# Attention and expert layer on one core: the second pair's x operands are issued eight slots later, behind six project blocks

## The chip, the cores and the metric

The kernel runs on one core of a Trainium2 chip. A core has TensorE (PE, the matmuls; PEld is its weight load), VectorE (DVE), ScalarE (ACT), GpSimd (POOL) and SyncE (SP, which here only issues DMAs). Each of them works through its own instructions in the order in which they were written; semaphores tie them together. The metric is the device time of one execution, in microseconds (us). One execution was also profiled, and the rows below are from it.

## The reference

Two layers follow each other. The first is attention with a learned bias (4 batches, 8 heads, 576 positions, 64 wide), the second a feed-forward layer on its 2304 tokens:

```
attn = softmax(scale * q @ k.T + bias(|i - j|)) @ v        # x: 2304 tokens x 512
h = x @ w_in                                               # 512 -> 2048
g = s * max(h, 0)**2 + b
out = g @ w_out                                            # 2048 -> 512
```

All is float32. The kernel multiplies in a reduced format (fp32r) and keeps the precision by splitting each operand into a high part and a low part, so that each product is three matmuls: high x high, high x low, low x high.

## The kernel before

The attention part fills the first 261 us; it is left as it is, but for two sums at its very end. The feed-forward part follows and is laid out in **slots**. An **item** is a pair of a weight group g (4 of them, 512 of the 2048 hidden columns each) and a token pair p (3 of them, 768 tokens each, which are two blocks of 384 columns). `items` (L465) is their order: (0, 0), (0, 1), (0, 2), (1, 2) and so on, twelve in all. The text calls p = 0, 1, 2 the first, second and third pair, and the items with them the first, second and third item.

The product with w_in is done by a Strassen scheme: 7 products in place of 8, on sums of blocks of x (T1 to T4, `X_SUMS`) and of w (S1 to S4). Each of the 7 needs an **x operand**, numbered 1 to 7: a block of x or one of the sums T1 to T4, split by `x_hi` (L593, on ACT, two instructions) and `x_lo` (L596, on DVE, two instructions). `x_sum` (L582) makes a sum, two instructions on DVE. `store_x` writes an operand to DRAM for later items, `load_x` reads a pair's x.

An item is two halves of seven slots, 14 slots in all. In slot T the loop at L1104 issues, in this order: one `product` (L625, six matmuls of 384 columns), in the order 1, 6, 5, 7, 2, 3, 4; then, by `SHARE`, some **project blocks** of the half before (`project`, L732: three matmuls of 512 columns each, twelve blocks a half); then `fire(T)`, which issues all that was put down for that slot with `at(slot, fn, prio)`, by priority (0 first, x work has 2). The four banks of PSUM hold a: products 1 and 2, b: 5 and 3, c: 6, d: 7 and 4. The work behind a half is `quad_posts` (L640), slots 1 to 9 after the half's start: ACT copies bank a (L657, slot 1), DVE adds c (L661, slot 2), adds b (L666, slot 3, the text calls it **v**), adds d (L669, slot 4); then relu (L680, L687), square, scale (L699), a high part (L707) and a low part (L716) for each of four blocks, which `project` reads. Product 3 adds into bank b in slot 5 of a half and so has to wait until v has read it. `evict` takes a finished output block from PSUM, on ACT for the first weight group.

The first item has no project blocks of a half before it, so its 14 slots are 84 matmuls of 384 columns and nothing else. The x operands of the first pair are made ahead of it (`prep`). Those of the second pair were made by `fresh_x(0, 1, ...)` in slots 6 to 14, that is while the first item runs, and those of the third pair by `fresh_x(1, 2, ...)` in slots 20 to 28, while the second item runs. Decoding of the next weight group (`fresh_w`, L491 to L501) lies beside it, on ACT, POOL and DVE.

```
        for o, name in ((6, "T1"), (7, "T2"), (9, "T3"), (12, "T4")):
        for i, m in enumerate(ORDER):
            o = base + (7 + i if i > 0 else 6)      # x_hi at o, x_lo at o + 1
    SHARE = (0, 4, 0, 0, 4, 0, 4)
```

## Time and profile before

| what | value |
|---|---|
| median of 3 runs | 648.07 us (647.71 to 653.99) |
| the profiled execution | 650.64 us |
| its span, first to last instruction | 648.9 us |
| PE busy | 631.1 us, 97% |
| DVE busy | 511.4 us, 79% |
| ACT busy | 450.9 us, 69% |
| mean granted clock of PE | 0.994 |

The profile names an instruction by its line, its engine and its tiles (out<-in); a start is counted from the first instruction of the span, "idle before" is how long the engine stood still ahead of it, and the arrow behind it names what it waited for. Matmuls are pipelined: they start closer together than one lasts, so a rate is read from the starts. In a group of equal instructions the time runs from the first start to the last end. The granted clock is given as a share of full speed: 1.00 is 2.4 GHz, 0.50 is 1.2 GHz.

### The profile page before, as it was taken

Reading aid. Unit: us, or ns where it says so; the run is one execution under the profiler, and the core shown is the slowest. Engines: PE = TensorE matmul, PEld = TensorE weight load, DVE = VectorE, ACT = ScalarE, POOL = GpSimd, SP = SyncE. Lnnn points to the kernel's source line nnn. Section 1 sums busy time; section 2 is a strip of 40 time slices with the busy share of each in tenths; the row PEclk is TensorE's granted clock in tenths of the full one; section 3 lists DMA queues with packets and bytes.
Section 4 is the critical chain, followed back from the end, with each engine's and each line's share of the span. In section 5 each row is a group of like instructions: output and inputs, shape, how many; then the busy total and the mean of one; then the engine's idle time right before and its main releaser. Section 6 shows DMA issues by size and latency. Waiting matters only on the chain.

```text
span 648.9 us, 14523 instructions
## 1 busy us (share of the span) xinstructions
PE 631.1 (97%) x5418; PEld 511.6 (79%) x5418; DVE 511.4 (79%) x1093; ACT 450.9 (69%) x945; POOL 165.6 (26%) x196
## 2 busy tenths in 40 slices
PE   8999999999999999979999999999999999999997
PEld 5667666666666666879898899999888999998886
DVE  7988889999999988897887566698686698575542
ACT  7988787888888788687676685576574665655540
POOL 7991423345697524010010100010100100000000
PEclk9999999999999999979999999999999999999999
DMA  6988777775776565693522445421627210718112
GB/s 187 327 249 248 260 245 236 246 235 183 255 245 220 170 205 159 219 368 110 223 92 89 168 164 177 164 88 34 239 95 251 90 58 1 268 48 280 62 48 98
DMA packets 51058, 115.27 MB, mean 178 GB/s; under 512 B 10156, under 2 KB 18860, under 8 KB 50988
## 3 DMA queue, kind: packets, MB, share of 16 engines
q1 hardware_dynamic: 50652, 114.08, 52.6%
q8 instruction: 43, 0.70, 0.4%
q10 hardware_dynamic: 208, 0.26, 0.1%
q14 instruction: 27, 0.22, 0.1%
q0 software_dynamic: 128, 0.00, 0.0%
HBM read 83.59 MB, written 30.14 MB: 175 GB/s over the span
## 4 chain that ended last, share of the span: by engine, by line
PE 75%; DMA 7%; POOL 5%; ACT 5%; DVE 4%; issue 3%; SPq 1%; DVEq 0%; ACTq 0%; POOLq 0%
PE o L741 31%; PE hps L635 27%; PE bps L168 5%; PE xps L437 5%; PE sps L275 4%; PE tps L348 3%; ACT pr L308 3%; DMA qt<-in_q_dram 2%; DMA kt<-in_k_dram 2%; DVE tt L297 1%; DMA rs<-rt 1%; POOL kr L248 1%; DMA big<-in_moe_w_in_dram 1%; DVE pt L378 1%; ACT pt L376 1%
## 5 line engine op out<-in xcount | busy, mean ns | idle before, releaser
L741 PE MATMUL o<-wo,gt 128*128 128x512 f32 x864 | 209.2, 392 | 0.0
L635 PE MATMUL hps<-x,wi 128*128 128x384 f32 x1008 | 190.7, 340 | 3.3 <-DVE h L666 3.3
L635 PEld LDWEIGHTS hps<-x,wi 128*128 128x128 f32 x1008 | 180.8, 190 | 10.0 <-DVE h L666 3.6
L741 PEld LDWEIGHTS o<-wo,gt 128*128 128x128 f32 x864 | 161.2, 188 | 31.3
L308 ACT ACTIVATE pr<-tt,mn 128x576 f32<-128x576 f32 x144 | 110.7, 770 | 35.4 <-DVE mn L297 35.2
L297 DVE CUSTOM_DVE_ANT_0 tt<-sps,bt 128x576 f32<-128x576 f32 x128 | 91.4, 751 | 8.4 <-PE sps L275 6.7
L348 PEld LDWEIGHTS tps<-ident,pr 64*128 64x128 f32 x1216 | 44.8, 137 | 44.2 <-issue 18.7
L437 PE MATMUL xps<-pt,vt 128*64 128x256 f32 (+1 forms) x512 | 76.0, 418 | 1.0 <-PE xps L437 1.0
L275 PE MATMUL sps<-kr,qr 64*128 64x288 f32 x768 | 73.2, 307 | 1.0 <-POOL kr L248 0.8
L348 PE MATMUL tps<-ident,pr 64*128 64x64 f32 x1216 | 56.7, 229 | 5.2 <-ACT pt L376 2.8
L275 PEld LDWEIGHTS sps<-kr,qr 64*128 64x128 f32 x768 | 58.8, 186 | 2.4 <-POOL kr L248 1.0
L699 ACT ACTIVATE h<-h,sb 128x384 f32<-128x384 f32 x72 | 50.8, 706 | 12.0 <-DVE h L695 10.8
L493 POOL TENSOR_SCALAR wf<-wf 128x512 f32<-128x512 f32 x16 | 13.0, 813 | 160.8 <-ACT wf L491 160.6
L378 DVE COPY pt<-tps 128x512 f32<-128x512 f32 x64 | 43.9, 685 | 9.1 <-PE tps L348 8.8
L680 ACT ACTIVATE h<-hps 128x384 f32<-128x384 f32 x24 | 11.7, 487 | 54.5 <-PE hps L635 54.5
L437 PEld LDWEIGHTS xps<-pt,vt 128*64 128x64 f32 x512 | 31.3, 136 | 21.3 <-issue 9.4
L716 DVE TENSOR_TENSOR gt<-h,gt 128x384 fp32r<-128x384 f32 x72 | 40.0, 557 | 6.1 <-ACT gt L707 6.0
L168 PE MATMUL bps<-f,pt__125 128*32 128x79 f32 (+44 forms) x640 | 39.7, 390 | 2.0 <-POOL f L137 1.2
L707 ACT ACTIVATE gt<-h 128x384 fp32r<-128x384 f32 x72 | 37.9, 526 | 2.3
L135 DVE TENSOR_SCALAR f<-lg,thr 128x432 f32<-128x432 f32 (+9 forms) x68 | 39.3, 659 | 0.0
L168 PEld LDWEIGHTS bps<-f,pt__125 128*32 128x32 f32 x640 | 24.1, 109 | 17.7 <-issue 6.4
L376 ACT ACTIVATE pt<-tps 128x512 f32<-128x512 f32 x64 | 36.8, 575 | 0.0
(145 smaller groups left out, 823.6 us busy)
## 6 DMA issues: line engine op xcount, KB each, us to landing
x<-xs SPq DMA_DIRECT2D x24, 768.0 KB
bias<-stg SPq DMA_DIRECT2D x36, 295.5 KB
xs<-x SPq DMA_DIRECT2D x12, 768.0 KB
bt<-bias SPq DMA_DIRECT2D x7, 1152.0 KB
kt<-in_k_dram SPq DMA_DIRECT2D x16, 464.0 KB
wd<-in_moe_w_out_dram SPq DMA_DIRECT2D x12, 512.0 KB
x<-xt SPq DMA_DIRECT2D x28, 192.0 KB
qt<-in_q_dram SPq DMA_DIRECT2D x16, 320.0 KB
```

Of the source, the lines that this page charges most:

```text
L168: nc.tensor.matmul(pb[32 * c:32 * c + 32, base + a:base + b], w2bd, mov, start=True, stop=True)
L275: nc.tensor.matmul(o, a, b, start=(i == 0), stop=(i == 2))
L297: nc.vector.tensor_tensor_reduce(tt.rearrange("p (a b) -> p a b", a=2), ps[x][:, :, 0:HALF], bias.rearrange("p (a b) -> p a b", a=2), -1.0 ...
L308: nc.scalar.activation(pr[:, x], tts.pop((n, x)), AF.Exp, bias=mn[:, x:x + 1], scale=-1.0, accum_out=sums[p][:, col // 3, col % 3:col % 3 ...
L348: nc.tensor.matmul(outs[r], src[d], ident[d, d], is_transpose=True, start=start, stop=True, skip_group_check=not start)
L376: nc.scalar.activation(o, i, AF.Copy)
L378: nc.vector.tensor_copy(o, i)
L437: nc.tensor.matmul(o, vt[:, 4 * x + kb, :], pt[:, kb, x, c], start=(i == 0), stop=(i == 4))
L635: nc.tensor.matmul(ps, w_ops[m][:, w, k, s], xo[p, m][:, x, k], start=(first and i == 0), stop=(i == 5), skip_group_check=not first)
L699: return lambda: nc.scalar.activation(tmp[fo, j], tmp[fo, j], AF.Identity, bias=b_, scale=s_)
L716: nc.vector.tensor_tensor(lo, tmp[fo, j], hi, op=ALU.subtract)
L741: nc.tensor.matmul(os_t[t], gt[:, a, tok], w[:, b], start=(fo == 0 and i == 0), stop=(fo == 3 and i == 2))
```

## The change

The second pair's operands are now issued in slots 12 to 19 by a new list of (slot, sum or operand), the third pair's in slots 23 to 30. T1 of the second pair is issued ahead of the last step of the attention part. A new helper `x_make` issues the two high parts and the two low parts of an operand in one slot. At slot 14, where the second item starts, six project blocks of the first item's first half are issued ahead of its product 1, those of fo = 1 first; the other six follow three at a time in slots 16 and 18. `project` therefore starts an output block with whichever of its blocks comes first. The loads of the third pair's x go from slot 16 to slot 19, and the first six decode steps of the second weight group from slots 15 to 20 to slots 19 to 22. What is computed stays the same.

```diff
@@ -729,17 +729,21 @@
 
     BLOCKS = [(t, fo) for fo in (0, 1) for t in range(3)] + [(t, fo) for t in range(3) for fo in (2, 3)]
 
+    begun = set()
+
     def project(n, j, k):
         g, p = items[n]
         t, fo = BLOCKS[k]
-        if fo == 0:
+        begin = (n, j, t) not in begun
+        if begin:
+            begun.add((n, j, t))
             os_t[t] = ps_o.tile([128, DM], F32, tag="o", name="o")
         gt = gts[n, fo, j]
         tok = slice(128 * t, 128 * t + 128)
         w = w_outs[fo]
         for i, (a, b) in enumerate(((0, 0), (0, 1), (1, 0))):
             nc.tensor.matmul(os_t[t], gt[:, a, tok], w[:, b],
-                             start=(fo == 0 and i == 0), stop=(fo == 3 and i == 2))
+                             start=(begin and i == 0), stop=(fo == 3 and i == 2))
         if (t, fo) in ((2, 0), (2, 1), (2, 2), (2, 3)):
             free_g.append(gts.pop((n, fo, j)))
 
@@ -971,6 +975,13 @@
         for e in range(2):
             x_lo(0, m, e, x_free[e])
 
+    def x_make(q, m, free):
+        x_new(q, m)
+        for e in range(2):
+            x_hi(q, m, e)
+        for e in range(2):
+            x_lo(q, m, e, free)
+
     next(att)
     for a in range(KB):
         load_x(1, a, 0, 2 * CH if a < KB - 1 else CH)
@@ -989,6 +1000,11 @@
         prep(m)
     product(0, 0, 1, False)
     product(0, 0, 6, False)
+    mix["acc"] = [tp.tile([128, 640 if i < 3 else 576], F32, tag="vn" if i < 3 else "tt", name=f"acc{i}")
+                  for i in (0, 1, 3, 4, 5)]
+    sums1 = [t[:, 0:CH] for t in mix["acc"]]
+    x_sum(1, "T1", 0, nc.vector, sums1)
+    x_sum(1, "T1", 1, nc.vector, sums1)
     next(att)
     store_xt(NP - 1)
     copy_x()
@@ -1006,8 +1022,8 @@
     free_g.extend(op.tile([128, 2, CH], F32R, name=f"gt{i}") for i in range(9))
     free_x.append(op.tile([128, 2, 2, CH], F32R, name="x7"))
     s2 = op.tile([128, 2, 2, 128], F32, name="s2")
-    mix["acc"] = [tp.tile([128, 640 if i < 3 else 576], F32, tag="vn" if i < 3 else "tt", name=f"acc{i}")
-                  for i in range(6)]
+    mix["acc"].insert(2, tp.tile([128, 640], F32, tag="vn", name="acc2"))
+    sums1.append(mix["acc"][2][:, 0:CH])
     ps_o = ctx.enter_context(tc.tile_pool(name="ps_o", bufs=4, space=PSUM, reuse_waits="tile"))
     fulls = [tp.tile([128, 576], F32, tag="rb", name=f"f{i}", bufs=2)[:, 0:512] for i in range(2)]
     free_f[:] = fulls + new_f
@@ -1015,35 +1031,27 @@
                         for i in range(2)]
     raws = [big[:, i] for i in range(4)]
     free_raw[:] = raws
-    x_free[:] = [[t[:, 0:CH] for t in mix[e]] for e in ("acc", "acc2")]
 
     for n in range(1, NI + 1):
         for j in range(2):
             for t, o in enumerate((5, 7, 7)):
                 at(14 * n + 7 * j + o, lambda n=n, j=j, t=t: evict(n - 1, 1 - j, t), 0)
 
-    def fresh_x(n, q, free):
-        base = 14 * n
-        for a in range(KB) if q > 1 else ():
-            at(base + 2, lambda a=a: load_x(q, a))
-        for o, name in ((6, "T1"), (7, "T2"), (9, "T3"), (12, "T4")):
-            for e in range(2):
-                at(base + o, lambda name=name, e=e: x_sum(q, name, e, nc.vector, free))
-        for i, m in enumerate(ORDER):
-            o = base + (7 + i if i > 0 else 6)
-            at(o, lambda m=m: x_new(q, m))
-            for e in range(2):
-                at(o, lambda m=m, e=e: x_hi(q, m, e))
-            for e in range(2):
-                at(o + 1, lambda m=m, e=e: x_lo(q, m, e, free))
-            if isinstance(X_OPS[m], str):
-                at(o + 2, lambda m=m: store_x(q, m))
+    def fresh_x(q, free, slots):
+        for o, e in slots:
+            for x in range(2):
+                if isinstance(e, str):
+                    at(o, lambda e=e, x=x: x_sum(q, e, x, nc.vector, free))
+            if not isinstance(e, str):
+                at(o, lambda e=e: x_make(q, e, free))
+                if isinstance(X_OPS[e], str):
+                    at(o + 2, lambda e=e: store_x(q, e))
 
     def fresh_w(g):
         base = 42 * (g - 1)
         first = g == 1
         if first:
-            passes = [15 + k for k in range(6)] + [28 + k // 2 for k in range(6)]
+            passes = [19 + (2 * k) // 3 for k in range(6)] + [28 + k // 2 for k in range(6)]
         else:
             passes = [base + 8 + (22 * k) // 12 for k in range(12)]
         passes += [base + 33 + k for k in range(12)]
@@ -1085,8 +1093,11 @@
     for i, m in enumerate(ORDER):
         if isinstance(X_OPS[m], str):
             at(4 + i // 2, lambda m=m: store_x(0, m), 1)
-    fresh_x(0, 1, x_free[0])
-    fresh_x(1, 2, x_free[1])
+    fresh_x(1, sums1, ((12, 1), (13, "T2"), (14, 6), (15, 5), (15, "T3"), (16, 7), (17, 2), (18, "T4"), (18, 3), (19, 4)))
+    for a in range(KB):
+        at(19, lambda a=a: load_x(2, a))
+    fresh_x(2, [t[:, 0:CH] for t in mix["acc2"]],
+            ((23, "T1"), (23, 1), (25, "T2"), (25, 6), (26, 5), (26, "T3"), (27, 7), (28, 2), (28, "T4"), (29, 3), (30, 4)))
     for g in range(1, NG):
         fresh_w(g)
     for n in range(2, NI - 1):
@@ -1101,14 +1112,19 @@
                     at(o + 4, lambda p1=p1, m=m: split_lo(p1, m))
 
     SHARE = (0, 4, 0, 0, 4, 0, 4)
+    AHEAD = 6
     for T in range(14 * NI + 15):
         n, r = divmod(T, 14)
         s, i = divmod(r, 7)
+        if T == 14:
+            for k in (3, 4, 5, 0, 1, 2):
+                project(0, 1, k)
         if n < NI and T >= 4:
             p = items[n][1]
             product(n, s, ORDER[i], s == 1 and n + 1 < NI and items[n + 1][1] != p)
         if 0 < n <= NI:
-            for k in range(sum(SHARE[:i]), sum(SHARE[:i + 1])):
+            share, k0 = ((0, 0, 3, 0, 3, 0, 0), AHEAD) if T < 21 else (SHARE, 0)
+            for k in range(k0 + sum(share[:i]), k0 + sum(share[:i + 1])):
                 project(n - 1, 1 - s, k)
         fire(T)
     sched.__exit__(None, None, None)
```

Three places in the new order carry the prediction. The first is DVE in the first item, up to v of its second half (L666). Before, sums into acc tiles and the low parts of x7 and x0 (operands 1 and 6 of the second pair) stand ahead of it:

```order
L585 TENSOR_TENSOR acc2_5389<-wd_5187,acc0_5387 128x384
L585 TENSOR_TENSOR acc3_5390<-wd_5187,acc1_5388 128x384
L598 TENSOR_TENSOR x7_5385<-wd_5187,x7_5385 128x384 x2
L716 TENSOR_TENSOR gt2_5378<-h2_5263,gt2_5378 128x384
L661 TENSOR_TENSOR h0_5261<-hps_5455,h0_5261 128x384
L716 TENSOR_TENSOR gt3_5379<-h1_5262,gt3_5379 128x384
L585 TENSOR_TENSOR acc4_5391<-wd_5187 128x384
L585 TENSOR_TENSOR acc5_5392<-wd_5187 128x384
L598 TENSOR_TENSOR x0_5180<-acc2_5389,x0_5180 128x384
L598 TENSOR_TENSOR x0_5180<-acc3_5390,x0_5180 128x384
L666 TENSOR_TENSOR h0_5261<-hps_5469,h0_5261 128x384
```

Now, at the same place:

```order
L716 TENSOR_TENSOR gt0_5383<-h2_5263,gt0_5383 128x384
L714 SCALAR_TENSOR_TENSOR gt1_5384<-h2_5263,sb_122,gt1_5384 128x384
L716 TENSOR_TENSOR gt2_5385<-h2_5263,gt2_5385 128x384
L661 TENSOR_TENSOR h0_5261<-hps_5449,h0_5261 128x384
L716 TENSOR_TENSOR gt3_5386<-h1_5262,gt3_5386 128x384
L666 TENSOR_TENSOR h0_5261<-hps_5461,h0_5261 128x384
```

Eight instructions of x work have left the piece, and v follows the low part of gt3 at once.

The second is ACT around slots 13 to 16 of the changed kernel; x0 is operand 6 and x1 operand 5 of the second pair, and hps_5533 is bank a of the second item, which its product 1 in slot 14 fills:

```order
L699 ACTIVATE h1_5262<-h1_5262,sb_122 128x384
L707 ACTIVATE gt6_5389<-h1_5262 128x384
L687 ACTIVATE h0_5261<-h0_5261 128x384
L594 ACTIVATE x0_5180<-acc3_5335 128x384
L594 ACTIVATE x0_5180<-acc4_5336 128x384
L657 ACTIVATE h2_5263<-hps_5533 128x384
L690 ACTIVATE h0_5261<-h0_5261 128x384
L699 ACTIVATE h0_5261<-h0_5261,sb_122 128x384
L707 ACTIVATE gt7_5390<-h0_5261 128x384
L594 ACTIVATE x1_5181<-acc0_5333 128x384
L594 ACTIVATE x1_5181<-acc1_5334 128x384
```

Before, all high parts of the second pair up to x5 stood ahead of the copy of that bank; now x1 and those after it stand behind it.

The third is PE from slot 13 on, in the changed kernel (o are output blocks, wi and wo the weights, x7, x0 and x1 operands 1, 6 and 5 of the second pair):

```order
L635 MATMUL hps_5470<-x6_5186,wi4_1014 128x384 x6
L745 MATMUL o_5512<-wo01_1016,gt0_5383 128x512 x3
L745 MATMUL o_5516<-wo01_1016,gt0_5383 128x512 x3
L745 MATMUL o_5520<-wo01_1016,gt0_5383 128x512 x3
L745 MATMUL o_5512<-wo00_1015,gt2_5385 128x512 x3
L745 MATMUL o_5516<-wo00_1015,gt2_5385 128x512 x3
L745 MATMUL o_5520<-wo00_1015,gt2_5385 128x512 x3
L635 MATMUL hps_5533<-x7_5392,wi1_1008 128x384 x6
L635 MATMUL hps_5550<-x0_5180,wi6_1009 128x384 x6
L635 MATMUL hps_5568<-x1_5181,wi5_1010 128x384 x6
```

Before, the first project block stood behind the product on x0; now six blocks (18 matmuls) stand ahead of the product on x7, and the products on x7, x0 and x1 come right behind each other.

## Rows read from the trace of the kernel before

**Rows 1.** The page, busy time: us, share of the span, instructions.

```profile
PE 631.1 (97%) x5418; PEld 511.6 (79%) x5418; DVE 511.4 (79%) x1093; ACT 450.9 (69%) x945; POOL 165.6 (26%) x196
```

**Rows 2.** Waits of PE, whole span: us in total, times, longest.

```profile
PE hps L635 <- DVE h L666: 3.3, 1, 3.3
PE tps L348 <- ACT pt L376: 2.8, 5, 1.1
```

**Rows 3.** Timeline of PE: start us, us, instruction, count, idle before it.

```profile
257.86 2.16 PE L437 MATMUL xps<-pt,vt 128*64 128x256 f32 x16 [0.97 <-PE xps L437]
...
265.20 10.91 PE L635 MATMUL hps<-x,wi 128*128 128x384 f32 x60
279.44 7.20 PE L635 MATMUL hps<-x,wi 128*128 128x384 f32 x24 [3.33 <-DVE h L666]
286.47 2.92 PE L741 MATMUL o<-wo,gt 128*128 128x512 f32 x12
289.23 2.96 PE L635 MATMUL hps<-x,wi 128*128 128x384 f32 x16
...
326.42 2.27 PE L635 MATMUL hps<-x,wi 128*128 128x384 f32 x12
328.53 2.92 PE L741 MATMUL o<-wo,gt 128*128 128x512 f32 x12
```

**Rows 4.** Windows of 2 us: busy us of each engine, then the granted clock.

```profile
276.00:278.00 2.00, 0.11 (x1) 0.00 (x0) 1.63 (x5) 2.00 (x5) 0.00 (x0) 1.00 0.95 317
...
282.00:284.00 2.00, 2.00 (x8) 2.00 (x7) 2.00 (x5) 1.97 (x5) 0.00 (x0) 0.50 1.06 438
...
286.00:288.00 2.00, 2.00 (x11) 1.74 (x10) 2.00 (x6) 1.97 (x5) 0.60 (x1) 1.00 1.02 427
```

**Rows 5.** Timeline of ACT ahead of the hole.

```profile
271.87 0.92 ACT L594 ACTIVATE x<-wd 128x384 fp32r<-128x384 f32 x2
272.70 0.70 ACT L699 ACTIVATE h<-h,sb 128x384 f32<-128x384 f32 x1
...
274.27 0.47 ACT L657 ACTIVATE h<-hps 128x384 f32<-128x384 f32 x1
274.64 0.51 ACT L690 ACTIVATE h<-h 128x384 f32<-128x384 f32 x1
...
275.93 0.52 ACT L707 ACTIVATE gt<-h 128x384 fp32r<-128x384 f32 x1
276.36 2.57 ACT L594 ACTIVATE x<-acc 128x384 fp32r<-128x384 f32 x6
```

**Rows 6.** Timeline of DVE ahead of the hole.

```profile
276.48 0.56 DVE L716 TENSOR_TENSOR gt<-h,gt 128x384 fp32r<-128x384 f32 x1 [0.37 <-ACT gt L707]
...
277.89 1.02 DVE L598 TENSOR_TENSOR x<-acc,x 128x384 fp32r<-128x384 f32 x2
278.83 0.55 DVE L666 TENSOR_TENSOR h<-hps,h 128x384 f32<-128x384 f32 x1
```

**Rows 7.** Timeline of DVE, single rows of the stretch from 265 to 324.

```profile
265.32 0.42 DVE L443 TENSOR_TENSOR rb<-xps,rb 128x256 f32<-128x256 f32 x1 [1.00 <-PE xps L437]
...
290.78 0.55 DVE L666 TENSOR_TENSOR h<-hps,h 128x384 f32<-128x384 f32 x1
...
296.35 0.62 DVE L684 SCALAR_TENSOR_TENSOR h<-h,sb 128x384 f32<-128x384 f32 x1 [3.62 <-ACT h L680]
...
298.55 1.02 DVE L585 TENSOR_TENSOR acd<-wd 128x384 f32<-128x384 f32 x2
...
311.99 0.62 DVE L684 SCALAR_TENSOR_TENSOR h<-h,sb 128x384 f32<-128x384 f32 x1 [2.16 <-ACT h L680]
...
323.94 0.55 DVE L666 TENSOR_TENSOR h<-hps,h 128x384 f32<-128x384 f32 x1
```

**Rows 8.** Window: busy us of PE, PEld, DVE, ACT, POOL; clock; DMA.

```profile
291.00:324.00 33.00, 33.00 (x167) 29.90 (x167) 26.94 (x55) 23.21 (x48) 1.91 (x3) 1.00 0.47 168
```

**Rows 9.** Timeline of SP: the loads of the third pair's x.

```profile
288.92 5.11 SPq L571 DMA_DIRECT2D wd<-xt  x8
```

## The prediction

> **What bounds it now.** I read the page first: TensorE (PE) is busy for 97% of the span [rows 1], so only time in which PE stands still, or runs slowly, can be won. The waits of PE come next: the largest single one of the whole span is 3.3 us, L635 waiting for DVE's L666 [rows 2]; all others of note lie in the attention part, which is left alone. PE's own timeline places it: sixty matmuls from 265.20 end at 276.11, PE stands for 3.33 us, and the next 24 start at 279.44 [rows 3]. From 289.23 on I find no further hole. Last the windows: over the hole the granted clock falls from 1.00 to 0.50, that is from 2.4 to 1.2 GHz, and is back at 1.00 before 286 to 288 is out [rows 4].
>
> What the hole costs in all: 24 matmuls of 384 columns take 286.47 - 279.44 = 7.03 us, where 24 at full clock would take 24 x 0.176 = 4.22 (twelve take 328.53 - 326.42 = 2.11) [rows 3]. So 2.81 us is lost to the clock, and the bill is 3.33 + 2.81 = **6.14 us**, 0.95% of 648.07. That is the whole prize.
>
> Why the hole is there: product 3 of the first item's second half (slot 12) adds into the bank that the add of L666 (called v here) reads, and v stands on DVE behind the second pair's x work. It starts at 278.83, behind a low part (L716, 276.48), two sums and two x low parts [rows 6], and that L716 waits for a chain on ACT that two x high parts (271.87 to 272.70) have pushed back [rows 5].
>
> **The change, part by part.**
>
> *T1 moved ahead.* Two sums of 0.47 us each now stand before L443, where DVE waits 1.00 us for PE [rows 7]. They fit; cost 0. Without that cover they would cost 0.94 once.
>
> *x operands leave slots 6 to 11 (hole 1).* ACT loses 272.70 - 271.87 = 0.83 us ahead of v's chain [rows 5]. L707 then ends at 275.93 + 0.52 - 0.83 = 275.62, L716 starts 0.03 later, v 0.47 after that at 276.12, ends at 276.67, and PE follows 0.06 later (279.44 against 278.83 + 0.55 in rows 3 and 6): 276.73. **Hole 1 is 276.73 - 276.11 = 0.62 us**, not 3.33. A hole of 0.97 at 257.86 left the clock alone, which is still at 1.00 from 276 to 278 [rows 3, 4], so I charge no clock.
>
> *Six project blocks first at slot 14.* The same matmuls in another place; their operands are made in slots 6 to 8, so nothing waits. PE: two products (2.11) to 278.84, 18 matmuls of 0.23 (12 take 289.23 - 286.47 = 2.76 [rows 3]) to 282.98, products 1 and 6 of the second item to 285.09. That gives the first two x operands 4.14 us of cover, and they are in time: operand 6, by the durations of rows 5 and 6, by about 0.3 us.
>
> *x operand 5 at slot 16 (hole 2, a new wait).* Its high part now stands on ACT behind the bank copy L657 of slot 15, and that copy waits for product 1 of the second item, which ends at 284.04. With PE's pipeline of about 0.16 the copy starts at 284.2. From the start of L657 to the first x high part behind it ACT takes 276.36 - 274.27 = 2.09 us over four instructions of the same kind [rows 5], so operand 5's first high part starts at 286.3, ends at 286.8, and PE starts at 286.87 instead of 285.09. The second matmul wants the low part: 0.55 on DVE plus 0.06, so 287.48. **Hole 2 is 286.87 - 285.25 = 1.62, then 0.28.** It is nearer to 0.97 than to 3.33, so I charge no clock again.
>
> *What is late next (hole 3).* From 287.48 on PE has 5 matmuls (to 288.36), 16 products (16.9) and 26 blocks of 0.69 (17.9) up to slot 33, plus some 0.2 of small waits: it wants product 3 of the third item at **323.3**, against 326.42 before [rows 3]. That product waits for v of the third item. DVE: from operand 5's low part at 286.87 eight instructions of 0.47 lead to v of the second item at 290.63, the same moment as before (290.78 [rows 7]). But before, DVE had by then done all 14 low parts and 8 sums of the second pair and two decode steps; now it has done 8 and 6 and none. It is behind by 8 x 0.47 + 0.94 = **4.7 us of work**. From there to v of the third item it was busy for 26.94 of 33 us [rows 8]; now it is 31.6. Bounds: if DVE never idles, v starts at 290.63 + 31.6 = 322.2 and ends at 322.8, no hole; with the 6.06 us of idle that the same stretch has before (3.62 and 2.16 of it on L684 [rows 7]), PE starts at 328.9, a hole of 5.5. I take the value from laying the new rows of ACT and DVE one behind the other with the durations of rows 5 to 7: since a slot now issues an operand's two high parts and two low parts together, DVE waits for ACT at five places, 0.7, 0.2, 0.4, 0.9 and 1.6 us, 3.8 in all. v then starts at 326.0, ends at 326.6, PE starts at 326.65: **hole 3 is 326.65 - 323.4 = 3.2 us.** That is nearly the old 3.33, so I let it drop the clock too, at the same 2.81.
>
> *x loads of the third pair three slots later.* SP issued its eight before in 5.11 us from 288.92 and the first sum on them came at 298.55 [rows 7, 9]. Now they are issued some 2 us later and the first sum, behind the backlog, stands near 303.6. Hidden; cost 0. If the cover were gone, a few us of DMA would fall on DVE in the same place as hole 3. Store and decode moves put no new transfer on the path; behind slot 33 both orders agree, and DVE and ACT have room again.
>
> *Sum.* Slot 33 starts at 326.65 against 326.42: +0.23. The old clock loss lies before that point and is in the 326.42; the new one lies behind it: +2.81. Together **+3.0 us**. The profiled execution took 650.64 (span 648.9 and 1.74 around it), so it would take 653.7; the median of the runs is 648.07, 2.57 below the profiled one, and I carry the difference over: **651.1 us**.
>
> **Rivals.**
>
> *Hole 3 without the drop.* 3.2 lies just under the 3.33 that dropped the clock, far over the 0.97 that did not, so it may go either way. Then +0.2: 648.3. The Trainium skill (TensorE: Matmul & The Clock Gate, The HAM clock gate) says that the chip's watch on PE runs free of the kernel, so that the same kernel loses differently from run to run. By that rule the drop comes in some executions and not in others, and the median is 648.3 where most go without; no run here shows it.
>
> *DVE catches up, no hole 3.* Decides at 0.5 us of idle on DVE from 290.6 to 322.2. For it: DVE then has work queued at all times. Against it: before, the same stretch idled for 6.06 us, and the low parts now follow their high parts at once. Slot 33 at 323.3, no drop: 3.1 us gained, 645.0.
>
> *Hole 2 drops the clock (slower).* 1.62 and 0.28 within 2.3 us lie between 0.97 and 3.33. If the point of decision is below about 1.7 us, slots 16 to 20 run at half clock for another 2.81, with hole 3 behind them as it is: 653.9.
>
> *The change does all it says.* Operands 1, 6 and 5 in time, no hole at all: 6.14 gained, 641.9. Against it stands L657 ahead of operand 5 in ACT's order.
>
> **Chances.** Forecast 0.50; no drop 0.22; DVE catches up 0.17; hole 2 drops the clock 0.07; no hole 0.04. Range: from the catch-up case less 1 us (the error of a walk over 60 us) to the slow case with 0.6 more, 644.0 to 654.5; it leaves out the no-hole case, and the tails. One per cent, about what a measurement of this kernel can tell from no change, is 6.5 us, and the cases run from -6.1 to +5.9: within 1% 0.92, faster 0.03, slower 0.05 (hole 3 at its bound with two drops).
>
> **What would show it.** Hole 1: a wait of L635 for L666 of some 0.6 us near 276.7. Hole 2: a wait of L635 for ACT's x (L594, the high part) near 286.9 of 1.6 us, with L657 just before on ACT. Hole 3: a wait of L635 for L666 near 326.6 with a granted clock of 0.5 in the 6 us behind it. If PE runs through slot 33 without a wait, the catch-up case holds; if the clock rows show 0.5 after 287, the slow one. Wrong altogether if PE shows a hole behind 330, or DVE waits for a DMA of the third pair's x.

## The result, and the profile after

| | before | with the change |
|---|---|---|
| median | 648.43 us (647.67 to 653.99) | 655.42 us (650.97 to 657.89) |
| ratio, 95% interval | | 1.0091, 1.0072 to 1.0110 |
| profiled execution | 650.64 us | 650.97 us, the lowest of all |
| its span | 648.9 us | 649.1 us |

The change makes the kernel slower, by 5 to 7 us (0.72% to 1.10% of 648.43). The forecast was 651.1, at most 654.5. By the tables of the two kernels each operand of the second pair moves six slots later (operand 1 from slot 6 to 12, operand 4 from 13 to 19), not eight as the title has it; the working goes by the slots themselves.

Waits of PE in the feed-forward part, with the change (us in total, times, longest). Where before had one [rows 2], there are three, two of them on the first line:

```profile
PE hps L635 <- DVE h L666: 4.6, 2, 3.8
PE hps L635 <- ACT x L594: 1.7, 1, 1.7
```

Their places, on the timeline of PE (start, us, instruction, idle before; L745 is L741 of before). Starts here are to be read against those of [rows 3] less 2.58 us, since the attention part ended that much sooner (first product at 259.19; 261.77 in the profile of before):

```profile
259.19 2.37 PE L635 MATMUL hps<-x,wi 128*128 128x384 f32 x12
...
274.14 2.38 PE L635 MATMUL hps<-x,wi 128*128 128x384 f32 x12 [0.85 <-DVE h L666]
276.36 4.28 PE L745 MATMUL o<-wo,gt 128*128 128x512 f32 x18
280.48 2.27 PE L635 MATMUL hps<-x,wi 128*128 128x384 f32 x12
284.41 1.74 PE L635 MATMUL hps<-x,wi 128*128 128x384 f32 x6 [1.66 <-ACT x L594]
...
325.27 3.62 PE L635 MATMUL hps<-x,wi 128*128 128x384 f32 x12 [3.79 <-DVE h L666]
```

The 3.33 us of [rows 3] are 0.85 now (hole 1), 1.66 are new at slot 16 (hole 2), and 3.79 are new at slot 33 (hole 3). ACT just ahead of hole 2: the bank copy L657 waits for PE, three more instructions follow, and only then operand 5's high part:

```profile
281.74 0.49 ACT L657 ACTIVATE h<-hps 128x384 f32<-128x384 f32 x1 [0.54 <-PE hps L635]
...
283.42 0.52 ACT L707 ACTIVATE gt<-h 128x384 fp32r<-128x384 f32 x1
283.85 0.92 ACT L594 ACTIVATE x<-acc 128x384 fp32r<-128x384 f32 x2
```

DVE at the end of the attention part (T1, and L443 behind it, now without the wait of [rows 7]), at the third pair's first sum, and in the last stretch ahead of hole 3:

```profile
261.65 1.02 DVE L585 TENSOR_TENSOR acc<-wd 128x384 f32<-128x384 f32 x2
262.73 0.42 DVE L443 TENSOR_TENSOR rb<-xps,rb 128x256 f32<-128x256 f32 x1
...
301.81 1.02 DVE L585 TENSOR_TENSOR acd<-wd 128x384 f32<-128x384 f32 x2
...
322.31 1.01 DVE L598 TENSOR_TENSOR x<-acd,x 128x384 fp32r<-128x384 f32 x2
323.25 0.68 DVE L498 SCALAR_TENSOR_TENSOR wf<-big,wf 128x512 uint32<-128x512 uint32 x1
323.97 0.69 DVE L501 SCALAR_TENSOR_TENSOR wf<-big,wf 128x512 uint32<-128x512 uint32 x1
324.58 0.55 DVE L666 TENSOR_TENSOR h<-hps,h 128x384 f32<-128x384 f32 x1
```

DVE goes straight from x work and decode steps (L498, L501) into v (L666), and PE starts 0.14 us after v ends. Windows (us, busy of PE, PEld, DVE, ACT, POOL, granted clock, DMA):

```profile
287.00:291.00 4.00, 3.98 (x21) 3.35 (x20) 4.00 (x9) 2.23 (x6) 0.61 (x1) 1.00 0.79 284
...
325.00:328.00 3.00, 2.73 (x9) 2.76 (x10) 2.05 (x5) 2.81 (x6) 0.00 (x0) 0.50 0.35 140
```

In this execution the clock is at half behind hole 3 alone (3.4 us from 324.7); in the profile of before it was at half for 6.8 us behind its one hole.

### The profile page after: what moved, and what is told of

It is laid out like the page before. It is cut to its first block, busy times and chain, and to the rows that moved or that the text cites. A ratio compares the mean times of both kernels' runs of the same rounds, so it can differ in the third digit from the quotient of the medians.

```text
span 649.1 us, 14520 instructions
## 1 busy us (share of the span) xinstructions
PE 630.6 (97%) x5418; PEld 509.5 (79%) x5418; DVE 512.1 (79%) x1093; ACT 451.4 (70%) x945; POOL 166.1 (26%) x196
## 4 chain that ended last, share of the span: by engine, by line
PE 71%; DVE 8%; ACT 7%; DMA 6%; issue 3%; POOL 3%; SPq 1%; DVEq 0%; ACTq 0%; POOLq 0%
PE o L745 28%; PE hps L635 23%; PE bps L168 6%; PE sps L275 5%; PE xps L437 5%; DMA qt<-in_q_dram 4%; PE tps L348 3%; ACT pr L308 3%; DVE tt L297 1%; DVE x L598 1%; DMA rs<-rt 1%; ACT pt L376 1%; DVE pt L378 1%; DMA kt<-in_k_dram 1%; POOL kr L248 1%
## 5 line engine op out<-in xcount | busy, mean ns | idle before, releaser
L745 PE MATMUL o<-wo,gt 128*128 128x512 f32 x864 | 209.2, 392 | 0.0
L635 PE MATMUL hps<-x,wi 128*128 128x384 f32 x1008 | 190.2, 339 | 6.5 <-DVE h L666 4.6
L635 PEld LDWEIGHTS hps<-x,wi 128*128 128x128 f32 x1008 | 179.2, 189 | 14.4 <-issue 4.7
L745 PEld LDWEIGHTS o<-wo,gt 128*128 128x128 f32 x864 | 161.2, 188 | 31.3
L493 POOL TENSOR_SCALAR wf<-wf 128x512 f32<-128x512 f32 x16 | 12.6, 787 | 158.1 <-ACT wf L491 157.8
L168 PE MATMUL bps<-f,pt__125 128*32 128x79 f32 (+46 forms) x640 | 40.3, 405 | 1.4 <-ACT stg L172 0.6
```

The costliest lines, as they stand in the source:

```text
L168: nc.tensor.matmul(pb[32 * c:32 * c + 32, base + a:base + b], w2bd, mov, start=True, stop=True)
L635: nc.tensor.matmul(ps, w_ops[m][:, w, k, s], xo[p, m][:, x, k], start=(first and i == 0), stop=(i == 5), skip_group_check=not first)
L745: nc.tensor.matmul(os_t[t], gt[:, a, tok], w[:, b], start=(begin and i == 0), stop=(fo == 3 and i == 2))
```

## The experiments

A time that is free of the attention part's length helps to compare profiles: the **feed-forward part**, the span less the start of the first L635. It is 648.9 - 261.77 = 387.1 us before and 649.1 - 259.19 = 389.9 with the change. All runs are in this table; "half clock" is where the one-microsecond windows behind 260 us show 0.5, leaving out the last 4 us of the span; waits of 0.15 us are left out.

| kernel | median us | ratio to before (95%) | feed-forward part | waits of PE in it | half clock behind |
|---|---|---|---|---|---|
| ctl_before | 649.99 | 1.0004 (0.9982 to 1.0025) | 387.1 | 3.32 | it, 6.8 us |
| rep_after | 654.50 | 1.0079 (1.0054 to 1.0103) | 391.2 | 0.85, 1.66, 3.78 | second, third, 3.4 each |
| change_again | 655.67 | 1.0079 (1.0049 to 1.0109) | 390.0 | 0.86, 1.66, 3.80 | third, 3.4 |
| x5_before_copy | 650.90 | 1.0024 (1.0002 to 1.0045) | 387.5 | 0.86, 3.77 | second, 3.4 |
| decode_later | 650.64 | 1.0020 (0.9999 to 1.0042) | 387.0 | 0.86, 1.66, 1.04 | second, 3.4 |
| both_fixes | 647.27 | 0.9952 (0.9928 to 0.9975) | 383.4 | 0.85, 1.03 | none |
| both_fixes_third_earlier | 645.18 | 0.9927 (0.9899 to 0.9956) | 382.7 | 0.86 | none |
| sums_on_gpsimd | 656.12 | 1.0084 (1.0050 to 1.0117) | 390.8 | 0.86, 1.66, 1.20, 1.96 | second, fourth, 3.4 each |
| no_blocks_ahead | 659.44 | 1.0141 (1.0096 to 1.0186) | 394.5 | 0.85, 2.75, 1.38, 3.38 | second, fourth, 3.4 each |
| only_blocks_ahead | 649.71 | 1.0004 (0.9981 to 1.0028) | 386.1 | 3.32 | it, 3.4 |
| third_pair_early | 658.59 | 1.0125 (1.0092 to 1.0158) | 394.9 | 0.86, 1.66, 2.29, 2.44 | second, fourth, 3.4 each |
| wait_filled | 653.69 | 1.0054 (1.0033 to 1.0074) | 391.0 | 0.86, 0.62, 3.78 | third, 6.8 |
| third_wait_filled | 653.87 | 1.0052 (1.0028 to 1.0076) | 389.6 | 0.86, 1.66, 0.60 | second, 3.4 |
| before_filled | 648.39 | 0.9970 (0.9951 to 0.9989) | 384.6 | 0.57 | none |
| both_waits_filled | 652.46 | 1.0035 (1.0013 to 1.0057) | 388.5 | 0.85, 0.62, 0.60 | none |

**Controls.** Before and the change, unchanged, beside the other kernels; the change again with the third group.

> The kernel before, unchanged, to see by span and mean clock of each execution how often its one hole (3.33 us) costs the clock. Theory A (a hole of this length drops the clock in some executions and not in others): the mean clock of the executions has two or more levels, near 0.997 to 1.0 and near 0.994, and the time goes with it, about 648 and 651. Theory B (the clock has nothing to do with the spread): one level of clock and a spread of times all the same. Median 648.4.

> The changed kernel, unchanged. Its profile had three holes on PE (0.85, 1.66, 3.79 us) and one clock drop of 3.4 us, and took 650.97, while the median of its executions is 655.4. Theory A: hole 2 and hole 3 each drop the clock in some executions, for 3.4 or 6.8 us, so the mean clock runs from 0.997 (one short drop) to 0.990 (two long ones) and each 0.005 of it costs about 3 us. Theory B: the holes themselves are longer in the slower executions, at the same clock. Median 655.

> The change, unchanged, once more beside the three kernels of this call: waits of PE of 0.85, 1.66 and 3.78 us as in its two profiles so far, a granted clock of 0.995 or less over the span in most executions (two stretches at half clock), about 654.5 us where before is 649.6. A rival to the reading that two stretches at half clock are the rule: most executions show 0.997 (one stretch) and the time is near 651.5 us.

The change again, timeline of PE and windows, from rep_after:

```profile
287.03 0.44 PE L635 MATMUL hps<-x,wi 128*128 128x384 f32 x1 [1.66 <-ACT x L594]
...
328.95 3.47 PE L635 MATMUL hps<-x,wi 128*128 128x384 f32 x12 [3.78 <-DVE h L666]
```

```profile
289.00:292.00 3.00, 3.00 (x9) 2.32 (x8) 3.00 (x7) 2.76 (x7) 0.61 (x1) 0.50 0.70 287
...
330.00:333.00 3.00, 3.00 (x10) 2.88 (x9) 2.66 (x7) 2.86 (x6) 0.00 (x0) 0.50 0.01 3
```

The same holes, to 0.01 us, but here hole 2 takes the clock down too, and the feed-forward part is 1.3 us longer than in the first profile. The profile of change_again shows one drop again.

The mean clock of each execution, attention part included, says more than three profiles. Of the 102 executions of before beside these runs none is above 0.997: the 31 that reach it have a median of 648.7 us, the 20 at 0.992 or less 652.1. Of 29 executions of the change none is above 0.997 either: 6 reach it, with 653.5 us, 8 are at 0.992 or less, with 657.0. So the clock goes with the time in both kernels, though not in steps as ctl_before's theory A had it, and on average it is the same in both, 0.994.

**Hole 2 alone: operand 5 one slot earlier**, ahead of the bank copy.

```
-    fresh_x(1, sums1, ((12, 1), (13, "T2"), (14, 6), (15, 5), ...
+    fresh_x(1, sums1, ((12, 1), (13, "T2"), (14, 6), (14, 5), ...
```

> Operand 5 of the second pair is issued in slot 14 in place of 15, so that its two high parts stand on ACT ahead of the bank copy L657 that waits for PE. One number changed. My theory: hole 2 (1.66 and 0.2 us) is gone, hole 3 stays at 3 to 4 us, slot 33 starts 2 us earlier; 2 us faster than the changed kernel, and up to 4.8 us faster where hole 2 used to drop the clock: 650.5 to 653.4. Rival (DVE is short of time up to slot 33 whatever is done in front): hole 3 grows by what hole 2 gives back, 655.

```profile
283.61 3.31 PE L635 MATMUL hps<-x,wi 128*128 128x384 f32 x18
...
325.96 3.75 PE L635 MATMUL hps<-x,wi 128*128 128x384 f32 x12 [3.77 <-DVE h L666]
```

On the timeline of PE the three products run through as x18; hole 2 and its drop are gone and hole 3 is as long as ever. So hole 2 comes from ACT's order, and its time is not given back at hole 3: slot 33 starts 63.60 us after the first product, 66.08 in the change. v depends on PE's earlier products and moves along with them.

**Hole 3 alone: the last six decode steps of the second weight group later**, in slots 31 and 32 (three each) in place of 28 to 30.

```
-            passes = [19 + (2 * k) // 3 for k in range(6)] + [28 + k // 2 for k in range(6)]
+            passes = [19 + (2 * k) // 3 for k in range(6)] + [31 + k // 3 for k in range(6)]
```

> The changed kernel with the second six decode steps of the next weight group moved from slots 28 to 30 to slots 31 and 32, behind v of the third item on DVE. Same work, only its place. My theory: hole 3 is made by what DVE has queued ahead of v in slots 28 to 30; without six decode steps of 0.4 to 0.7 us there (3.5 us) it shrinks from 3.8 to below 1 us, and no clock drop follows it: 3 us of hole and 1.4 to 2.8 us of clock, 649.5 to 651. Hole 2 stays. Rival (the time only moves): a hole of the same size opens later, at slot 35 or at the weights of the fourth item, 655.

```profile
278.11 2.38 PE L635 MATMUL hps<-x,wi 128*128 128x384 f32 x12 [0.86 <-DVE h L666]
...
326.35 1.22 PE L635 MATMUL hps<-x,wi 128*128 128x384 f32 x6
328.61 1.30 PE L635 MATMUL hps<-x,wi 128*128 128x384 f32 x6 [1.04 <-DVE h L669]
```

```profile
325.38 0.54 DVE L666 TENSOR_TENSOR h<-hps,h 128x384 f32<-128x384 f32 x1
...
327.91 0.55 DVE L669 TENSOR_TENSOR h<-hps,h 128x384 f32<-128x384 f32 x1
```

Timeline of PE at hole 1 and at slot 33, then DVE at slot 33. The 0.86 is hole 1. At slot 33 PE no longer waits for v at all: the 3.8 us are gone, and 1.04 for L669 have come in, ahead of which DVE now does decode steps. No drop follows. Hole 3 is made by work that stands ahead of v in DVE's queue.

**Both.** The two edits together; then, with them, the third pair's loads, sums and operands one slot earlier (loads at 18, operands from 22).

> The change with both single repairs at once: operand 5 made one slot earlier (ahead of the bank copy on ACT) and the decode steps of the second weight batch 3 slots later. Theory (the three waits are separate, and each wait that is broken up or gone also keeps its clock drop away): waits of PE in the feed-forward part are 0.85 us near its start, none behind ACT's operand 5, and about 0.9 and 1.0 us (sum at most 2.2) at slot 33; no stretch at half clock in the feed-forward part. The feed-forward part then lasts 387.0 (the run decode_later) - 1.9 (1.66 + 0.15 gone, with what follows) - 1.3 (one drop) = 383.8 us, against 387.1 before: 3 us faster, about 646.5 us where before is 649.9. Rival (PE arriving 1.9 us earlier at slot 33 only waits so much longer there, since DVE's work is what sets that point): slot 33 waits 3.8 us in sum, with a drop, 387 us, about 650 us.

> Both repairs (operand 5 one slot earlier, the second batch's decode steps 3 slots later) and the third pair's loads, sums and operands one slot earlier. Theory (DVE's queue ahead of slot 33 is all that still holds PE there): the waits of 0.9 and 1.0 us at slot 33 go, one wait of 0.3 us at most comes near 294 us, no half clock in the feed-forward part; it lasts 383.4 - 0.5 to 383.4 - 1.9, so 381.5 to 382.9 us, and the time is about 646 us where before is 649.5. Rival (one slot earlier brings the two pairs' operands together already, as three slots do): waits of over 1 us near 292 us, and 647.5 us or more.

Waits of PE in the feed-forward part of both_fixes. The 0.9 for L666 is hole 1 (0.85), not a wait at slot 33, as the two expectations above have it; only the 1.0 for L669 is there:

```profile
PE hps L635 <- DVE h L669: 1.0, 1, 1.0
PE hps L635 <- DVE h L666: 0.9, 1, 0.9
```

The first kernel lasts 383.4 in its feed-forward part where 383.8 was expected, the second 382.7, with 0.86 us of hole 1 as its only wait of note. The gains add up, which the rival denied: against the change's 1.0083 (the mean of its three ratios), the first edit alone gains 0.6%, the second alone 0.6%, both 1.3%. Holes 2 and 3, with their drops, are thus worth more than the whole slowdown. At 645.18 us, 0.9927 of before, the second beats both kernels: the change's idea was sound, and two places of its tables were not.

**Is DVE short of time, or is it the order?** The third pair's eight sums go to GpSimd (`fresh_x` hands an engine to `x_sum`, `nc.gpsimd` for the third pair).

> The change with the eight sums of the third pair's x operands (T1 to T4, L585) on GpSimd instead of DVE, at the same slots. It takes some 4 us of DVE's work out of slots 23 to 28. Theory (the wait at slot 33 is made by what stands right ahead of L666 on DVE, the decode steps with their waits on ACT): the wait falls by only about 1 us, to 2.7 us (laying the rows one behind the other), hole 2 stays at 1.7 us, and the time is 0.5 to 1 us under the change's, about 653.5 us where the change has 654.5. Rival (DVE simply has too much to do between slots 21 and 33, and any work taken from it shortens the wait by as much): the wait at slot 33 is gone (under 0.5 us), no clock drop behind it, and the time is 3.8 + 1.4 = 5 us under the change's, about 649.5 us.

Timelines of GpSimd and of DVE in this kernel:

```profile
299.99 2.75 POOL L585 TENSOR_TENSOR acd<-wd 128x384 f32<-128x384 f32 x2
302.70 2.75 POOL L585 TENSOR_TENSOR acd<-wd,acd 128x384 f32<-128x384 f32 x2
305.42 2.49 POOL L585 TENSOR_TENSOR acd<-wd 128x384 f32<-128x384 f32 x2
315.69 2.33 POOL L585 TENSOR_TENSOR acd<-wd,acd 128x384 f32<-128x384 f32 x2
```

```profile
304.50 1.36 DVE L714 SCALAR_TENSOR_TENSOR gt<-h,sb,gt 128x384 fp32r<-128x384 f32 x1
305.79 1.24 DVE L495 TENSOR_SCALAR wf<-wf 128x512 uint32<-128x512 uint32 x1
307.06 1.39 DVE L498 SCALAR_TENSOR_TENSOR wf<-big,wf 128x512 uint32<-128x512 uint32 x1
...
317.14 2.18 DVE L598 TENSOR_TENSOR x<-acd,x 128x384 fp32r<-128x384 f32 x2 [0.97 <-ACT x L594]
```

```profile
311.92 2.35 PE L635 MATMUL hps<-x,wi 128*128 128x384 f32 x12 [1.20 <-DVE h L666]
...
329.77 3.73 PE L635 MATMUL hps<-x,wi 128*128 128x384 f32 x12 [1.96 <-DVE h L666]
```

Neither theory is met. Hole 3 falls to 1.96 (2.7 and none were expected), but a wait of 1.20 comes in at slot 26, and no time is won. While GpSimd works, DVE's instructions take up to three times as long: L714 1.36 (0.61 elsewhere in the same kernel), L495 1.24 (0.42), L498 1.39 (0.69), two L598 2.18 (1.02). DVE gave up eight instructions and got much of their time back as waiting inside others. L676 at 303.21, which reads one of its two operands from PSUM, kept its 0.55 meanwhile. So the test doesn't part the two theories; decode_later does: there DVE has the same work in another order, and hole 3 is gone.

**Which part of the change brings what.** The change without its six blocks ahead of the second item; and before with these blocks alone.

> The change without its six project blocks ahead of the second item: the blocks stand where they stood before, the x operands are made at the change's slots. Theory (the six blocks are what covers the operands that are still being made, so that without them PE waits for operands 6 and 5 in turn): waits of about 0.85, 3 and 1.6 us between 276 and 300 us and 3.1 us at slot 33, 4.5 us more idle than the change, and at least two clock drops: about 659 us where the change has 654.5. Rival (the operands are in time by themselves and the blocks only shift work): no new wait, 654.5 us.

> The kernel before with only the six project blocks moved ahead of the second item; x operands, loads and decode steps as before. Theory (the wait of 3.3 us that the change breaks up hangs on DVE's queue ahead of the third block, which the order of PE's work does not touch; the later waits come from the later operands and decode steps alone): one wait of 3.3 to 3.6 us for L666 at the same place, none near slots 16 and 33, time within 1 us of before. Rival (the six blocks by themselves make the later waits, since PE comes to the next products sooner or later than DVE): waits near 287 and 326 us as in the change, time 3 to 5 us over before.

Timeline of PE in no_blocks_ahead:

```profile
284.60 1.83 PE L635 MATMUL hps<-x,wi 128*128 128x384 f32 x6 [2.75 <-ACT x L594]
...
299.20 0.44 PE L635 MATMUL hps<-x,wi 128*128 128x384 f32 x1 [1.38 <-ACT x L594]
```

The blocks are cover for the late operands: without them PE waits 2.75 us for operand 6 (slot 15) and 1.38 for operand 4 (slot 20), not 5 as was expected, and the kernel is at 659.44 (two executions). By themselves they move nothing: the old hole is 3.32 us, in its old place. The new waits come from the operands and what was moved with them.

**The third pair three slots earlier**, as before had it (its loads at 16, its operands from 20), the rest as in the change. In this kernel the loads overwrite the second pair's x before its operands 2, 3 and 4 have been made, so these are made from the third pair's x, and wait for it.

> The change with the third pair's x loads, sums and operands three slots earlier, where the kernel before had them (loads at slot 16, operands at 20 to 27); the rest as in the change. Theory (laying the rows one behind the other: the move later is needed once the second pair's operands are made in slots 12 to 19, since DVE and ACT would have both at once): the wait at slot 33 is gone, but new waits of about 3.6 us near 291 us and 2.4 us near 312 us come in, 3.9 us more idle than the change, each with its drop: about 658 us. Rival (the move later is what makes the wait of 3.8 us, and taking it back only takes that wait away): no wait from 290 us on, 3.8 + 1.4 us less than the change, about 649.3 us.

ACT in this kernel, and PE:

```profile
295.82 0.52 ACT L594 ACTIVATE x<-wd 128x384 fp32r<-128x384 f32 x1 [5.64 <-DMA wd<-xt]
```

```profile
296.40 0.44 PE L635 MATMUL hps<-x,wi 128*128 128x384 f32 x1 [2.29 <-ACT x L594]
...
316.65 3.80 PE L635 MATMUL hps<-x,wi 128*128 128x384 f32 x12 [2.44 <-DVE h L666]
```

Hole 3 is gone, 2.29 and 2.44 us are new, the kernel is at 658.59. The 2.29 is partly the edit's own fault: ACT waits 5.64 us for the load. So this run doesn't decide how much of hole 3 the later slots make. It does show why they are later: one buffer (wd) holds a pair's x, and the third pair's loads cannot go ahead of the second pair's last reads in slot 18.

**What the clock costs, without touching a wait.** Repeats of products whose operands are long there are put into PE's queue right ahead of a wait. The wait stays as it is, and PE isn't idle in it. At slot 16 they are six repeats of operand 6's products in the bank that operand 5 starts anew; at a v (slot 12 of before, slot 33 of the change) they go to a spare bank:

```
+        if T == 33:
+            spare = ps_o.tile([128, DM], F32, tag="o", name="spare")
+            for r in range(14):
+                nc.tensor.matmul(spare, gts[1, 0, 0][:, 0, 0:128], w_outs[0][:, 0], ...)
```

> The change with six repeats of operand 6's products put in front of operand 5's first products in slot 16: they go into the bank that the true products start anew, so they add PE work only where PE stood idle (6 x 0.19 = 1.1 us of the 1.66 us), and operand 5's products start no later and no sooner. The wait itself stays, its idle part shrinks to about 0.5 us. Theory (the idle stretch of 1.66 us is what takes the clock down at 289 us): no stretch at half clock near 289 us, the feed-forward part lasts 391.2 - 1.3 = 389.9 us, and the median is 1.0 to 1.5 us under that of the change in this call, about 653.3 us. Rival (the drop there hangs on something other than the idle stretch): half clock near 289 us as before, time equal to the change's, 654.5 us.

> The kernel before with 12 spare products (L741's shape, 128x512, 0.23 us each, of a high part that is long made, into a PSUM bank that nothing else uses yet) put into PE's queue right ahead of its wait of 3.3 us at slot 12. They run where PE stood idle, and the true products start no later. Theory (a wait of PE also costs a stretch at half clock behind it, which in the profile of before was 6.83 us long and cost 2.8 us, and in other executions is half as long): no half clock near 279 us, the feed-forward part lasts 387.1 - 2.8 = 384.3 us, and the median is 1.4 to 2.8 us under before, about 647.5 us where before is 649.6. Rival (the clock's part is small, and what counts is the idle time alone): no change within 0.5 us.

> The change with 14 such spare products (3.2 us) right ahead of its wait of 3.8 us at slot 33, the one of 1.7 us at slot 16 left as it is. Theory (each wait pays for its own stretch at half clock): no half clock near 325 to 330 us; one near 289 us in some executions; the feed-forward part lasts 388.5 us without that one and 389.8 with it, and the median is 1.4 to 2.8 us under the change's, 652.5 to 654 us where before is 649.6. Rival (idle time alone counts): the change's time, 655 us. The spare bank shifts the turn of the o banks once, which can hold the project blocks of slot 36 by some 0.6 us.

> The change with both waits filled: six repeats ahead of operand 5 at slot 16 and 14 spare products at slot 33. Every true product still waits as long as in the change; PE is only not idle meanwhile. Theory: no half clock in the feed-forward part, which lasts 389.9 - 1.4 = 388.5 us; against before_filled (384.3) that leaves 4.2 us, the three waits' 6.3 us less the 3.3 us of before and what follows them; the time is about 651.7 us where before is 649.6, so that 3.5 us or so of the change's 5 to 7 us over before is waiting and the rest is clock. Rival (the clock has no large part): 655 us as the change. A third outcome would say that something else than waits and clock is at work: no half clock, and still 653.5 us or more.

PE in before_filled, then PE and the windows in both_waits_filled (L1110, L636 and L1130 are the repeats; L640 and L671 are L635 and L666):

```profile
276.53 2.92 PE L1110 MATMUL spare<-wo,gt 128*128 128x512 f32 x12
280.02 4.79 PE L635 MATMUL hps<-x,wi 128*128 128x384 f32 x24 [0.57 <-DVE h L666]
```

```profile
283.84 1.21 PE L636 MATMUL hps<-x,wi 128*128 128x384 f32 x6
...
322.57 3.33 PE L1130 MATMUL spare<-wo,gt 128*128 128x512 f32 x14
326.50 2.34 PE L640 MATMUL hps<-x,wi 128*128 128x384 f32 x12 [0.60 <-DVE h L671]
```

```profile
288.00:292.00 4.00, 4.00 (x21) 3.38 (x20) 4.00 (x9) 2.40 (x6) 0.61 (x1) 1.00 0.80 301
...
330.00:334.00 4.00, 4.00 (x22) 3.63 (x21) 3.95 (x8) 3.31 (x7) 0.96 (x1) 1.00 0.00 0
```

In before_filled 24 matmuls last 4.79 us, where [rows 3] has 7.20; in both_waits_filled the clock is at 1.00 behind both holes. This holds beyond the two profiles: 5 of 12 executions of before_filled and 7 of 12 of both_waits_filled have a mean clock of 0.999 or more, which none of those 102 of before and 29 of the change has. Read from the ratios, which share their runs of before: filling its hole gains before 0.30%, 1.9 us; filling hole 2 gains the change about 0.29%, hole 3 about 0.31%, both 0.48% (from 1.0083, the mean of its three ratios), 3.1 us, each with some 1.5 us of uncertainty. What is left is waiting alone: 652.46 - 648.39 = 4.1 us between the medians, 388.5 - 384.6 = 3.9 between the feed-forward parts. So the change costs **some 4 us more of waiting**. Its clock costs 3.1 - 1.9 = 1.2 us more than that of before by these ratios, which is not clear of their uncertainty; the mean clocks, 0.994 in both and 0.998 in both with the waits filled, show no difference.

## Why the prediction was wrong

*T1 moved ahead, cost 0*: right. L443 follows it without a wait, 262.73 - 259.19 = 3.54 us after the first L635; before it was 265.32 - 261.77 = 3.55 [rows 7].

*Hole 1, 0.62 us, no drop*: 0.85, and no drop in any profile.

*Six blocks first, nothing waits*: right; without them operand 6 would come 2.75 us late.

*Hole 2, 1.62 us behind L657*: 1.66, in its place and for its reason; the second matmul then started 0.59 us after the first (287.62 - 287.03 in rep_after), where 0.61 was laid out. **The price given to it was wrong.** "Nearer to 0.97 than to 3.33, so I charge no clock" took a place between two rows for an answer. Of the seven profiles that have the wait unfilled at 1.66, five show half clock behind it (rep_after, decode_later, sums_on_gpsimd, third_pair_early, third_wait_filled) and two don't. Where it comes it costs about 1 us: slot 33 starts 328.95 - 261.84 = 67.11 us after the first product in rep_after, 66.08 in the first profile. This is the rival that had 0.07. The time that it gave, 653.9, is near what was measured (1.0091 x 648.07 = 654.0), in part by luck: it charged 2.81 for this drop, and the waiting was too short by about 0.8.

The Trainium skill (TensorE: Matmul & The Clock Gate, The HAM clock gate), cited for the first rival, says that the watch on PE runs free of the kernel. The traces agree with it so far as one and the same wait of 1.66 us dropped the clock in five profiles and not in two.

*Hole 3, 3.2 us with a drop of 2.81*: the wait was 3.79, the drop 1.3 to 1.6. The wait is longer since v came later than worked out. From v of the second item to v of the third DVE took 36.44 us, where 35.4 was laid out:

```profile
288.14:324.58 36.44, 33.33 (x166) 29.40 (x164) 33.22 (x66) 26.13 (x55) 3.86 (x5) 1.00 0.55 201
```

Busy 33.22 (window of the change), not 31.6, and idle 3.2, not 3.8. Some of the additional 1.6 us are instructions beside GpSimd's L493: L495 0.84, L498 0.98 and a pair of L585 1.44 stand there, at 0.42, 0.69 and 1.02 elsewhere; before had one such pair in its stretch (L598, 1.43). The drop was too large because its 2.81 came from the profile of before, whose half clock lasted 6.8 us; behind hole 3 it lasts 3.4 in four of five profiles that have it. By rows: from slot 33 to the group behind its blocks the change took 331.49 - 325.27 = 6.22 us, and both_waits_filled 331.45 - 326.50 = 4.95.

*x loads later, hidden*: right. The first sum on them (301.81) waits for nothing.

*The sum*: +3.0 us for a profiled execution, and the first one shows 389.9 - 387.1 = +2.8. That is less of a success than it looks. Slot 33 starts 325.27 - 259.19 = 66.08 us after the first product, against 64.65 before: +1.43, not +0.23. The drop behind it costs 1.3, not 2.81. The two errors cancel; in executions in which hole 2 drops the clock as well, the sum is +4.0 (rep_after).

**The steps that failed are two terms of the sum.** *The waiting.* The +0.23 counts from a start of slot 33 that has the old drop's 2.81 in it; waiting alone was forecast to make it 0.23 + 2.81 = 3.0 us later. With the long waits filled, so that no drop comes in, it starts 326.50 - 260.47 = 66.03 us after the first product in both_waits_filled and 324.60 - 262.37 = 62.23 in before_filled: 3.8 us later (4.1 between the medians). Holes 3 and 1 were too small, by 0.6 and 0.2. *The clock.* Two drops of 2.81, one on each side, made nothing. The runs show one in before and, in most profiles, two shorter ones in the change, 0 to 1.2 us more in sum; hole 2's was put at nothing without a row that could decide it. Together that is 4 to 5 us, against 5.1 by the ratios of the later runs and 5.9 by the first one. What is left, up to 2 us, is not explained; the attention part alone varies by more.

*"The difference of 2.57 I carry over"* puts the +3.0 on the median, 648.07 + 3.0 = 651.1, and is sound only so far as the +3.0 is. It does not make a rule for single executions: before's profiled one lies 2.2 us over the 648.43 measured beside the change, the change's 4.45 us under its median. That 650.64 + 3.0 = 653.7 would have been nearer to 655.42 is luck: its base lies 2.2 us too high.

*The other rivals*: DVE does not catch up (against it 3.79 us), and hole 3 drops the clock in each profile in which it is unfilled and whole.

## What to carry to other kernels

Moving producers later to clear one engine's wait moves their backlog with them: walk on to the next instruction that stands behind them in the same queues, here the bank copy ahead of operand 5 and the decode steps ahead of v, and move these too. A wait of TensorE has two prices, the idle time and the clock behind it; the second varies from execution to execution and belongs into the sum as a chance, for waits well below the longest one too. The price of such a drop is not to be taken from one execution either, nor is a kernel's time: what is to be compared is medians taken side by side.

## What the runs showed of the hardware

*Which idle time drops the clock.* In the feed-forward parts of all these profiles waits of 0.57 to 1.38 us never did; 1.66 did in five of seven; 1.96, 2.44 and 2.75 did, and one of 2.29, in third_pair_early, did not; those from 3.3 us up always did. Half clock then lasted 3.4 us in most, and cost 1.3 to 1.6 us behind hole 3, but 6.8 us in before, ctl_before and wait_filled. Why it lasts twice as long there is not shown: only_blocks_ahead has the same wait of 3.32 us and 3.4 us of half clock.

*GpSimd and DVE.* DVE's instructions of 0.4 to 0.7 us took up to 1.5 us while GpSimd worked in sums_on_gpsimd. The Trainium skill (SBUF — State Buffer, Who interferes with whom) says that a DVE instruction with two inputs in SBUF contends with a GpSimd instruction that reads SBUF, that tensor_scalar in a two-port mode does so too, and that whichever comes later is blocked until the other has finished. The rows agree: L714, L498 and L598 have two such inputs, L495 is a tensor_scalar (in which mode, no run here shows), and all four were held (1.24 against 0.42 for the last); L676, with one input in SBUF and one in PSUM, was not (0.55).

*The attention part.* Its instructions are the same in all kernels but for T1, and yet the first product of the feed-forward part started anywhere from 259.2 to 265.3 us in these profiles. Six of the profiles show half clock in it, two for 10 us near 60 us (sums_on_gpsimd, only_blocks_ahead), four for 3.4. The rest of that spread is not explained here, and it is as large as the effect of the change.
